# Retention and two feed-forward layers: units of the retention taken in pairs, kind by kind

## The chip, the core and the metric

One core of a Trainium2 chip runs the whole program. Five engines work side by side, each through its own list of instructions in order: TensorE (PE, matmuls into PSUM banks), VectorE (DVE), ScalarE (ACT), GpSimd (POOL) and SyncE (SP, which here only starts DMA transfers). Engines wait for one another on semaphores. The metric is the time of one execution on the device in microseconds; three runs of the kernel before gave 588.07, 588.76 and 588.95 us.

## The reference

```python
def _attn_ref(q, k, v):                   # batch 2, heads 8, seq 768, head_dim 64
    gamma = 1.0 - 2.0 ** (-5.0 - np.arange(H))
    state = np.zeros((B, H, D, D))
    for t in range(S):
        state = gamma * state + outer(k[:, :, t], v[:, :, t])
        y[:, :, t] = D ** -0.5 * q[:, :, t] @ state
...
x = y as (1536 tokens, 512)
x = ((x @ w_a) * (x @ w_b)) @ w_out       # d_ff 1536
h = x @ w_in                              # d_ff 2048
out = np.maximum(0.01 * h, h) @ w_out2
```

The weights are stored in 64-bit floats; x, q, k and v in 32-bit floats.

## The kernel before, in words

The retention is computed in chunks of 128 positions. The 1536 positions (two sequences) are cut into three tiles of 512 positions, four chunks each, and the eight heads into four pairs of heads. One tile of one pair of heads is a **unit**; there are 12, numbered tile by tile, so that units 0 to 3 are the first tile. For a unit four kinds of matmul are run on PE:

- `scores` (L426): k times scaled q inside each chunk, into two PSUM banks (one per head). DVE multiplies each bank with the decay and the causal mask and writes it to SBUF as P (L443, two instructions of 128x512).
- `states` (L454): scaled k (`kd`) times v, into one bank (kv). DVE runs the chain of states through the chunks with three or four small instructions (cr, L476 and L478).
- `within` (L500): P times v, into the bank xp.
- `across` (L514): the spread states times scaled q, added onto xp. Then xp leaves as two tiles, x high (ACT, a rounding copy, L209) and x low (DVE, a subtraction, L210).

Around them stand `prep` (L406): ACT scales n (k in the other layout) to `kd` with two instructions (L415), and GpSimd scales q to `qs` (L419; DVE does it for units 0 and 1); and `spreads` (L483): ACT copies the unit's states into one of two buffers `wk`, whose other halves are zero (L495), so that two heads share one matmul.

Where a matmul has 32-bit operands the trace holds two records for it: 16 for the scores of a unit, 12 or 16 for its states, 16 within, 6 or 8 across.

The loop over u (L626) writes the order by hand, one unit at a time: scores and states of unit u+1, one step of the first weight block, within and across of unit u, spreads of u+1, prep of u+3, loads of u+8. In the last turn but one the spreads of unit 11 stand ahead of within and across of unit 10. Every engine keeps the program's order, so what one function issues on ACT or DVE stands behind all that was issued there before.

`loads` (L390) starts the four transfers q, k, n and v of a unit, 256 KB each, on SP's queue (the first k on ACT's). Each transfer waits on SP until the one eight before it has landed. The loads of units 0 to 6 are issued ahead of the loop. The tiles take slots of one pool of 81 slots of 2 KB per partition, as do kd, qs, P and x.

The weights come in raw blocks of 512 KB of 64-bit floats (`load_weights`, L236, four buffers) and are rounded to 32 bits: ACT makes two parts (`begin_weights`, L255 and L256), DVE joins them in four steps (`round_steps`: sign L270, min L272, shift L274, add L278). `want` then splits the rounded block into a high part (ACT, L209) and a low part (DVE, L210). Only block a0 is rounded inside the loop, in six calls of `micro`: begin; sign; min; shift; add; split. They come one a turn from u = 3 (`EARLY`) on. Its raw transfer is issued between the loads of units 4 and 5 (L614); the next ones are issued at the end of the turns from u = 3 on.

Behind the loop the first layer starts with `pa`: 36 matmuls that read x high, x low, a0 high and a0 low; the third one is the first that reads a0 low. While they run, block b0 is rounded and split, which the next 36 matmuls (pb) read.

Of the kernel before, what the change touches and what calls it, by code (L numbers as in the profile page):

```python
# [19 lines left out]
B, H, S, D = 2, 8, 768, 64  # L20
# [10 lines left out]
NSLOT = 81  # L31
NRAW = 4
NEXTRA = 10
EARLY = 3
NWARM = 7
COUNT = {"a": FF1, "b": FF1, "wo": FF1, "wi": FF2, "wq": FF2}
HALF = FF2 // 2
# [150 lines left out]
def retention_moe_kernel(ctx: ExitStack, tc: tile.TileContext, ins, out):  # L188
    nc = tc.nc
# [10 lines left out]
    def bank(name):  # L200
        return psum.tile([P, TT], F32, tag="ps", name=name)
# [4 lines left out]
    def split(src, name, new=slots.new):  # L206

        hi, lo = new(F32R, name + "h"), new(F32R, name + "l")
        nc.scalar.copy(hi, src)  # L209
        nc.vector.tensor_sub(lo, src, as32(hi))  # L210
        return hi, lo
# [24 lines left out]
    def load_weights():  # L236
        if at["load"] < len(order) and at["load"] < at["round"] + NRAW:
            kind, f = order[at["load"]]
            src, i = source[kind]
            t = rawp.tile([P, TT], I64, tag="raw", name=f"raw_{kind}{f}")  # L240
            nc.sync.dma_start(t, src[f, i])
            raws[kind, f] = t
            at["load"] += 1
# [128 lines left out]
    consts, chain, spread = [], [], []  # L372

    def attention_constants():
        for p in range(NPAIR):
            consts.append(ap.tile([P, P], F32, tag=f"cst{p}", name=f"cst{p}"))

        for p in range(NPAIR):
            chain.append([ap.tile([P, CPT, D], F32, tag=f"cr{p}{j}", name=f"cr{p}{j}") for j in range(2)])

        for i in range(2):
            spread.append(ap.tile([P, CPT, P], F32, tag=f"wk{i}", name=f"wk{i}"))
            nc.gpsimd.memset(spread[i][0:D, :, D:P], 0.0)
            nc.gpsimd.memset(spread[i][D:P, :, 0:D], 0.0)

    units = [(t, p) for t in range(NTILE) for p in range(NPAIR)]
    un = {}
    x = {}

    def loads(u):  # L390
        if u >= len(units):
            return
        t, p = units[u]
        d = un[u] = {}
        if u < NPAIR:
            nc.sync.dma_start(consts[p], grow[p])
        for name, src in (("q", qT), ("k", kT), ("n", kn), ("v", vn)):
            d[name] = slots.new(F32, f"{name}{u}")
            queue = nc.scalar if u == 0 and name == "k" else nc.sync
            queue.dma_start(d[name], src[t, p])  # L400
            if u == 0 and name == "q":
                nc.scalar.dma_start(small, dec)
            if u == 0 and name == "v":
                nc.sync.dma_start(causal, tri)

    def prep(u):  # L406
        if u >= len(units):
            return
        t, p = units[u]
        d = un[u]  # L410
        d["kd"] = slots.new(F32, f"kd{u}")
        for h in range(2):
            o = d["kd"].rearrange("p (j h d) -> p j h d", j=CPT, h=2)[:, :, h, :]
            i = d["n"].rearrange("p (j h d) -> p j h d", j=CPT, h=2)[:, :, h, :]
            nc.scalar.activation(o, i, AF.Copy, scale=small[:, 2 * p + h:2 * p + h + 1])  # L415
        d["qs"] = slots.new(F32, f"qs{u}")
        g = consts[p].rearrange("p (o t) -> p o t", o=1)

        (nc.vector if u < 2 else nc.gpsimd).tensor_mul(  # L419
            d["qs"].rearrange("p (j t) -> p j t", j=CPT),  # L420
            d["q"].rearrange("p (j t) -> p j t", j=CPT),
            g.to_broadcast([P, CPT, P]),
        )
        slots.done(2)

    def scores(u):  # L426

        if u >= len(units):
            return
        t, p = units[u]  # L430
        d = un[u]
        sc = [bank(f"sc{u}{h}") for h in range(2)]
        for j in range(CPT):
            c = slice(j * P, (j + 1) * P)
            for h in range(2):
                r = slice(h * D, (h + 1) * D)
                nc.tensor.matmul(sc[h][:, c], d["k"][r, c], d["qs"][r, c], start=True, stop=True)  # L437
        d["P"] = []
        m = causal.rearrange("p (o t) -> p o t", o=1)
        for h in range(2):  # L440
            pt = slots.new(F32, f"P{u}{h}")
            n = H + NPAIR + 2 * p + h
            nc.vector.scalar_tensor_tensor(  # L443
                pt.rearrange("p (j t) -> p j t", j=CPT),
                sc[h].rearrange("p (j t) -> p j t", j=CPT),
                small[:, n:n + 1],
                m.to_broadcast([P, CPT, P]),
                op0=ALU.mult,
                op1=ALU.mult,
            )  # L450
            d["P"].append(pt)
        slots.done(1)

    def states(u):  # L454
        if u >= len(units):
            return
        t, p = units[u]
        d = un[u]
        kv = bank(f"kv{u}")
        chunks = [t * CPT + j for j in range(CPT)]  # L460
        for j, c in enumerate(chunks):
            if c % CPB != CPB - 1:
                for h in range(2):
                    r = slice(h * D, (h + 1) * D)
                    s = slice(j * P + h * D, j * P + (h + 1) * D)
                    nc.tensor.matmul(
                        kv[r, j * D:(j + 1) * D], d["kd"][:, s], d["v"][:, s], start=True, stop=True
                    )
        own = chain[p][t % 2]
        for j, c in enumerate(chunks):  # L470
            if c % CPB == CPB - 1:
                continue
            o = own[:, j + 1] if j < CPT - 1 else chain[p][(t + 1) % 2][:, 0]
            n = kv[:, j * D:(j + 1) * D]
            if c % CPB == 0:
                nc.vector.tensor_copy(o, n)  # L476
            else:
                nc.vector.scalar_tensor_tensor(  # L478
                    o, own[:, j], small[:, H + p:H + p + 1], n, op0=ALU.mult, op1=ALU.add
                )  # L480
        slots.done(1)

    def spreads(u):  # L483

        if u >= len(units):
            return
        t, p = units[u]
        chunks = [t * CPT + j for j in range(CPT)]
        own = chain[p][t % 2]
        used = [c % CPB != 0 for c in chunks] + [False]  # L490
        runs = [(a, used.index(False, a)) for a in range(CPT) if used[a] and not (a and used[a - 1])]
        for a, b in runs:
            for h in range(2):
                r = slice(h * D, (h + 1) * D)
                nc.scalar.copy(spread[u % 2][r, a:b, h * D:(h + 1) * D], own[r, a:b])  # L495
        un[u]["S"] = spread[u % 2]

    cols = [slice(j * P, (j + 1) * P) for j in range(CPT)]

    def within(u):  # L500
        d = un[u]
        xp = d["x"] = bank(f"xp{u}")
        for j, c in enumerate(cols):
            for h in range(2):
                r = slice(h * D, (h + 1) * D)
                nc.tensor.matmul(
                    xp[r, c],
                    d["v"][:, j * P + h * D:j * P + (h + 1) * D],
                    d["P"][h][:, c],
                    start=j == 0,  # L510
                    stop=False,
                )

    def across(u):  # L514
        t, p = units[u]
        d = un.pop(u)
        xp = d["x"]
        later = [(t * CPT + j) % CPB != 0 for j in range(CPT)]
        for j, c in enumerate(cols):
            if later[j]:  # L520
                nc.tensor.matmul(xp[:, c], d["S"][:, j], d["qs"][:, c], start=False, stop=j == CPT - 1)  # L521
        x[t, p] = split(xp, f"x{u}")
        slots.done(4)


    h = {}
# [83 lines left out]
    for _ in range(NWARM):  # L610
        nc.tensor.matmul(wps, warm[:, 0:P], warm, start=True, stop=True)
    for u in range(1, 7):
        if u == 5:
            load_weights()  # L614
        loads(u)
    prep(0)
    def first_weights():
        begin_weights()
        yield
        yield from round_steps()  # L620
        yield
        want("a", 0)

    micro = first_weights()
    prep(1)
    for u in range(-1, len(units)):  # L626
        scores(u + 1)
        slots.tick()
        if u == 0:
            within(u)  # L630
        states(u + 1)
        slots.tick()
        if u >= EARLY:
            next(micro, None)
        if u + 1 == len(units) - 1:
            spreads(u + 1)
        if u > 0:
            within(u)
        if u >= 0:
            across(u)  # L640
        if u + 1 < len(units) - 1:
            spreads(u + 1)
        if u < 0:
            prep(2)
        else:
            prep(u + 3)
        loads(u + 8)
        if u + 8 >= len(units) - 1:
            load_weights()
        slots.tick()  # L650
    att.close()
# [276 lines left out]
```

## Time and profile before

| | us |
|---|---|
| median of 3 runs | 588.76 (588.07 to 588.95) |
| span of the profiled execution, first to last instruction | 587.1 |
| PE busy | 578.6 (99%) |
| DVE busy | 452.5 (77%) |
| ACT busy | 308.5 (53%) |
| POOL busy | 22.0 (4%) |

The page gives the span of the profiled execution; what lies around the span is in the median and not in the profile. Busy time counts an engine's instructions, not its waits. Matmuls overlap, so the start of one kind to the start of the next says more than a duration. The retention takes the first 50.27 us of the span; the two layers take the rest. In rows of a timeline the columns are the start and the length in us, the engine, the line, the operation, what it writes and reads, the shape and the count; the brackets hold how long the engine was idle before and what released it.

### The profile page before, as it was taken

How to read it: one execution, taken by the hardware profiler on the slowest of the kernel's cores; microseconds unless marked ns; L12 is line 12 of the kernel's file. 1: busy time of each engine (PE TensorE's matmuls, PEld its weight loads, DVE VectorE, ACT ScalarE, POOL GpSimd, SP SyncE). 2: the span in 40 equal slices, each digit the busy share in tenths (PEclk: the TensorE clock that was granted, in tenths of full speed). 3: DMA queues.
4: the chain of work that ended last, by engine and by line, in shares of the span. 5: the costliest groups of instructions: out<-in, count | busy, mean ns of one | idle time of the engine just before them, and what ended most of it. 6: DMA issues, size and time to landing. Idle time of an engine off the chain costs nothing.

```text
span 587.1 us, 8742 instructions
## 1 busy us (share of the span) xinstructions
PE 578.6 (99%) x3247; PEld 488.8 (83%) x3247; DVE 452.5 (77%) x937; ACT 308.5 (53%) x656; POOL 22.0 (4%) x32
## 2 busy tenths in 40 slices
PE   7999999999999999999999999999999999999997
PEld 5788788888888888888888888888888888888886
DVE  4795688889877788889999938657775766879992
ACT  4674446455354344547657356554633356788710
POOL 2430000000000000000000000000000000000000
PEclk9999999999999999999999999999999999999999
DMA  8991244555433343340014102213220000010111
GB/s 306 361 387 47 88 139 151 178 180 179 162 106 124 98 156 116 118 158 22 1 54 143 56 3 105 97 48 107 73 71 2 2 0 1 0 56 1 54 55 54
DMA packets 23050, 59.62 MB, mean 102 GB/s; under 512 B 2784, under 2 KB 4448, under 8 KB 23008
## 3 DMA queue, kind: packets, MB, share of 16 engines
q1 hardware_dynamic: 21600, 55.13, 28.0%
q0 software_dynamic: 1120, 3.67, 1.6%
q8 instruction: 25, 0.41, 0.3%
q10 hardware_dynamic: 288, 0.27, 0.1%
q14 instruction: 17, 0.14, 0.1%
HBM read 52.24 MB, written 6.82 MB: 101 GB/s over the span
## 4 chain that ended last, share of the span: by engine, by line
PE 91%; DMA 4%; DVE 3%; ACT 1%; issue 0%; SPq 0%; DVEq 0%
PE blk L216 11%; PE blk L215 11%; PE blk L217 11%; PE h L215 7%; PE h L216 7%; PE h L217 7%; PE pa L215 5%; PE pa L216 5%; PE pa L217 5%; PE pb L217 5%; PE pb L216 5%; PE pb L215 5%; DMA v<-in_vn 2%; PE xp L521 1%; DMA n<-in_kn 1%; PE sc L437 1%
## 5 line engine op out<-in xcount | busy, mean ns | idle before, releaser
L216 PE MATMUL blk<-form,form 128*128 128x512 f32 (+1 forms) x224 | 75.7, 338 | 0.0
L215 PE MATMUL blk<-form,form 128*128 128x512 f32 (+1 forms) x224 | 75.5, 337 | 0.0
L217 PE MATMUL blk<-form,form 128*128 128x512 f32 (+1 forms) x224 | 75.3, 336 | 0.0
L543 ACT COPY h<-pa 128x512 f32<-128x512 f32 x33 | 19.5, 590 | 84.6 <-PE pa L217 84.6
L779 ACT ACTIVATE g<-h 128x512 f32<-128x512 f32 x48 | 28.6, 597 | 62.2 <-PE h L217 62.2
L138 DVE TENSOR_TENSOR form<-g,form 128x512 fp32r<-128x512 f32 x112 | 57.3, 553 | 2.4 <-ACT form L132 0.7
L216 PE MATMUL blk<-forma,forma 128*128 128x512 f32 (+1 forms) x168 | 57.0, 339 | 0.4 <-DVE forma L138 0.4
L132 ACT CAST form<-g 128x512 fp32r<-128x512 f32 x112 | 52.6, 514 | 8.4 <-DVE g L113 6.4
L215 PE MATMUL blk<-forma,forma 128*128 128x512 f32 (+1 forms) x168 | 56.6, 337 | 0.0
L217 PE MATMUL blk<-forma,forma 128*128 128x512 f32 (+1 forms) x168 | 56.5, 336 | 0.0
L138 DVE TENSOR_TENSOR form<-wq,form 128x256 fp32r<-128x256 f32 x56 | 23.6, 421 | 35.5 <-ACT form L132 35.4
L215 PEld LDWEIGHTS blk<-form,form 128*128 128x128 f32 x224 | 42.5, 190 | 5.5
L216 PEld LDWEIGHTS blk<-form,form 128*128 128x128 f32 x224 | 42.5, 190 | 5.0
L217 PEld LDWEIGHTS blk<-form,form 128*128 128x128 f32 x224 | 42.3, 189 | 4.7
L138 DVE TENSOR_TENSOR forma<-h,forma 128x512 fp32r<-128x512 f32 x84 | 43.1, 553 | 0.8
L132 ACT CAST forma<-h 128x512 fp32r<-128x512 f32 x84 | 38.8, 511 | 0.0
L216 PEld LDWEIGHTS blk<-forma,forma 128*128 128x128 f32 x168 | 31.8, 189 | 4.6 <-DVE forma L138 0.9
L215 PEld LDWEIGHTS blk<-forma,forma 128*128 128x128 f32 x168 | 31.8, 190 | 4.1
L217 PEld LDWEIGHTS blk<-forma,forma 128*128 128x128 f32 x168 | 31.7, 189 | 3.5
L113 DVE TENSOR_TENSOR g<-g,g 128x512 f32<-128x512 f32 (+1 forms) x56 | 30.7, 571 | 3.6 <-ACT g L779 3.6
L546 DVE TENSOR_TENSOR h<-h,pb 128x512 f32<-128x512 f32 x33 | 22.5, 683 | 8.4 <-PE pb L217 5.4
L132 ACT CAST forma<-wo 128x256 fp32r<-128x256 f32 x42 | 17.1, 407 | 17.4 <-PE blk L217 13.2
(3091 smaller groups left out, 1447.3 us busy)
## 6 DMA issues: line engine op xcount, KB each, us to landing
raw_wi<-in_w SPq DMA_DIRECT2D x16, 512.0 KB, 3.2
raw_wq<-in_w SPq DMA_DIRECT2D x16, 512.0 KB, 3.4
raw_a<-in_wab SPq DMA_DIRECT2D x12, 512.0 KB, 3.2
raw_b<-in_wab SPq DMA_DIRECT2D x12, 512.0 KB, 3.4
raw_wo<-in_wo SPq DMA_DIRECT2D x12, 512.0 KB, 3.3
q<-in_qT SPq DMA_DIRECT2D x12, 256.0 KB, 5.2
n<-in_kn SPq DMA_DIRECT2D x12, 256.0 KB, 5.2
v<-in_vn SPq DMA_DIRECT2D x12, 256.0 KB, 5.3
```

The costliest lines, as they stand in the source:

```text
L113: queue.append((cost, lambda piece=piece: run(*(self.A(*x[1:], j)[piece] for x in (d, x0, x1)))))
L132: nc.scalar.copy(h, src)
L138: nc.vector.tensor_sub(*todo.pop(0))
L215: nc.tensor.matmul(ps, w[0], x[0], start=first, stop=False, skip_group_check=more)
L216: nc.tensor.matmul(ps, w[0], x[1], start=False, stop=False, skip_group_check=more)
L217: nc.tensor.matmul(ps, w[1], x[0], start=False, stop=last, skip_group_check=more)
L437: nc.tensor.matmul(sc[h][:, c], d["k"][r, c], d["qs"][r, c], start=True, stop=True)
L521: nc.tensor.matmul(xp[:, c], d["S"][:, j], d["qs"][:, c], start=False, stop=j == CPT - 1)
L543: nc.scalar.copy(h[t, f], pa)
L546: nc.vector.tensor_mul(h[t, f], h[t, f], pb)
L779: nc.scalar.activation(g[t, f], ps, AF.Lrelu, alpha=0.01)
```

## The change

From unit 4 (`SINGLE`) on, units are taken in pairs. A turn n of the loop has a group `now` and the following group `then`, of one unit up to unit 3 and of two units behind it. Scores of both units of `then` come first, then the states of both, then within for both units of `now`, then across for both. In a turn whose `then` is a pair, the preparation (`prep`) up to two units beyond `then` is issued between within and across; otherwise it stays at the end of the turn. The spreads of `then` follow across, but in the last turn that has a `then` they stand ahead of that preparation and of across. There are four spread buffers instead of two. The six steps of block a0 come two a turn, behind across and the spreads, from the turn of units 4 and 5 on. The raw transfer of a0 is issued behind the loads of unit 9; loads run seven units ahead of `now` instead of eight.

```diff
-        for i in range(2):
+        for i in range(4):
             spread.append(ap.tile([P, CPT, P], F32, tag=f"wk{i}", name=f"wk{i}"))
...
     for u in range(1, 7):
-        if u == 5:
-            load_weights()
         loads(u)
...
-    for u in range(-1, len(units)):
-        scores(u + 1)
+    groups = [[u] for u in range(SINGLE)] + [[u, u + 1] for u in range(SINGLE, len(units), 2)]
+    prepared = 2
+    for n in range(-1, len(groups)):
+        now = groups[n] if n >= 0 else []
+        then = groups[n + 1] if n + 1 < len(groups) else []
+        for u in then:
+            scores(u)
         slots.tick()
-        if u == 0:
-            within(u)
-        states(u + 1)
+        if n == 0:
+            within(0)
+        for u in then:
+            states(u)
         slots.tick()
-        if u >= EARLY:
-            next(micro, None)
-        if u + 1 == len(units) - 1:
-            spreads(u + 1)
-        if u > 0:
-            within(u)
-        if u >= 0:
-            across(u)
-        if u + 1 < len(units) - 1:
-            spreads(u + 1)
-        if u < 0:
-            prep(2)
-        else:
-            prep(u + 3)
-        loads(u + 8)
-        if u + 8 >= len(units) - 1:
-            load_weights()
+        if n > 0:
+            for u in now:
+                within(u)
+        last = n + 2 == len(groups)
+        if last:
+            for u in then:
+                spreads(u)
+        if len(then) == 2:
+            while prepared <= then[-1] + 2:
+                prep(prepared)
+                prepared += 1
+        for u in now:
+            across(u)
+        if not last:
+            for u in then:
+                spreads(u)
+        while prepared <= (then or now)[-1] + 2:
+            prep(prepared)
+            prepared += 1
+        if now and now[0] >= SINGLE:
+            next(micro, None)
+            next(micro, None)
+        for u in now:
+            loads(u + 7)
+            if u == 2:
+                load_weights()
+        if now and now[-1] + 7 >= len(units):
+            load_weights()
         slots.tick()
```

`spreads` takes buffer `u % 4` where it took `u % 2`.

## Rows read from the trace of the kernel before

**Rows 1.** The page, busy time of each engine: us, share, instructions.

```profile
PE 578.6 (99%) x3247; PEld 488.8 (83%) x3247; DVE 452.5 (77%) x937; ACT 308.5 (53%) x656; POOL 22.0 (4%) x32
```

**Rows 2.** The chain of waits, 10 to 30 us: start, length, what.

```profile
16.13 7.49 DMA n<-in_kn
...
26.72 1.02 PE xp L521 x6
```

**Rows 3.** Timeline of PE, 33 to 51 us.

```profile
33.47 0.94 PE L521 MATMUL xp<-qs,wk 128*128 128x128 f32 x6
34.34 1.16 PE L437 MATMUL sc<-qs,k 64*128 64x128 f32 x16
...
37.67 1.16 PE L437 MATMUL sc<-qs,k 64*128 64x128 f32 x16
...
43.69 1.16 PE L521 MATMUL xp<-qs,wk 128*128 128x128 f32 x8
...
50.27 0.47 PE L215 MATMUL pa<-x0h,a0h 128*128 128x512 f32 x1
...
50.81 0.40 PE L217 MATMUL pa<-x0h,a0l 128*128 128x512 f32 x1
```

**Rows 4.** Stretches: length, busy (PE, PEld, DVE, ACT, POOL; second PE alone), clock, DMA, GB/s.

```profile
30.00:45.00 15.00, 15.00 (x218) 13.09 (x216) 14.55 (x33) 10.54 (x28) 5.12 (x4) 1.00 0.97 370
...
584.20:587.10 2.90, 0.00 (x0) 1.00 0.50 176
```

**Rows 5.** Timeline of DVE, 31 to 50 us.

```profile
31.76 0.42 DVE L272 TENSOR_SCALAR a<-a 128x512 f32<-128x512 f32 x1
32.10 0.68 DVE L210 TENSOR_TENSOR x5l<-xp,x5h 128x512 fp32r<-128x512 f32 x1
...
37.99 0.68 DVE L278 CUSTOM_DVE_ANT_0 a<-a,low 128x1024 uint16<-128x1024 uint16 x1
38.59 0.69 DVE L210 TENSOR_TENSOR x7l<-xp,x7h 128x512 fp32r<-128x512 f32 x1
...
40.51 0.90 DVE L478 SCALAR_TENSOR_TENSOR cr<-cr,small,kv 128x64 f32<-128x64 f32 x3
41.33 0.69 DVE L210 TENSOR_TENSOR a0l<-a,a0h 128x512 fp32r<-128x512 f32 x1
42.00 0.69 DVE L210 TENSOR_TENSOR x8l<-xp,x8h 128x512 fp32r<-128x512 f32 x1
42.61 1.40 DVE L443 SCALAR_TENSOR_TENSOR P<-sc,small,causal 128x512 f32<-128x512 f32 x2
43.92 0.90 DVE L478 SCALAR_TENSOR_TENSOR cr<-cr,small,kv 128x64 f32<-128x64 f32 x3
...
49.95 0.69 DVE L210 TENSOR_TENSOR x10l<-xp,x10h 128x512 fp32r<-128x512 f32 x1 [1.56 <-ACT x10h L209]
```

**Rows 6.** Timeline of ACT, 23 to 50 us.

```profile
23.64 0.91 ACT L415 ACTIVATE kd<-n,small 128x256 f32<-128x256 f32 x2 [1.99 <-DMA n<-in_kn]
...
39.11 0.91 ACT L415 ACTIVATE kd<-n,small 128x256 f32<-128x256 f32 x2
39.92 0.60 ACT L209 CAST a0h<-a 128x512 fp32r<-128x512 f32 x1
...
41.86 0.83 ACT L495 COPY wk<-cr 64x256 f32<-64x256 f32 x2
42.72 0.91 ACT L415 ACTIVATE kd<-n,small 128x256 f32<-128x256 f32 x2
...
49.33 0.59 ACT L209 CAST x10h<-xp 128x512 fp32r<-128x512 f32 x1
```

**Rows 7.** Timeline of SP, loads of unit 11.

```profile
32.81 1.04 SPq L400 DMA_DIRECT2D q<-in_qT  x1
34.66 0.33 SPq L400 DMA_DIRECT2D k<-in_kT  x1
35.34 0.33 SPq L400 DMA_DIRECT2D n<-in_kn  x1
```

**Rows 8.** DMA issues, 35.2 to 35.6 us: count, KB each, us to landing.

```profile
n<-in_kn SPq DMA_DIRECT2D x1, 256.0 KB, 5.3
```

More of the change, by code (lines that the diff above doesn't have):

```diff
@@ L33 @@
 NEXTRA = 10
-EARLY = 3
+SINGLE = 4
 NWARM = 7
@@ L494, in spreads @@
                 r = slice(h * D, (h + 1) * D)
-                nc.scalar.copy(spread[u % 2][r, a:b, h * D:(h + 1) * D], own[r, a:b])
-        un[u]["S"] = spread[u % 2]
+                nc.scalar.copy(spread[u % 4][r, a:b, h * D:(h + 1) * D], own[r, a:b])
+        un[u]["S"] = spread[u % 4]
     cols = [slice(j * P, (j + 1) * P) for j in range(CPT)]
```

## Prediction

> **What bounds the kernel now.** The page comes first: TensorE (PE) is busy for 578.6 of 587.1 us [rows 1], so a change can win or lose only where PE waits or works inefficiently. The chain of waits shows where PE is not the chain: a DMA up to 23.6 us, ScalarE (ACT) up to 26.7, and from there PE [rows 2] until the retention ends at 50.27, where the first matmul of the first layer (pa) starts [rows 3]. Everything behind 50.27 is the same program in both kernels. So the sum is made at that point: what pa's matmuls lose or gain there is the result, if nothing behind gives it back.
>
> The table of engine times by stretch comes next: from 30 to 45 us PE is busy 15.00 of 15 us, VectorE (DVE) 14.55, and the DMA engines 0.97 of the time at 370 GB/s [rows 4]. Three resources run at their limit side by side. A unit takes PE 3.33 us (scores at 34.34 to scores at 37.67 [rows 3]); it takes DMA 1.05 MB / 370 GB/s = 2.8 us; it takes DVE 1.31 for P, 0.82 for the chain and 0.61 for x low, 2.74 us [rows 5], and in this stretch the steps of the first weight block besides. So little can be bought on PE alone.
>
> The timelines of single engines come last. ACT works in order, and one row shows what hurts there: the scaled keys kd of unit 5 stood 1.99 us waiting for the DMA of n [rows 6], and all that is queued behind on ACT (x high, the spreads) stood with them.
>
> **The change part by part.** *Raw block a0 later.* It is 0.52 MB, 1.4 us at 370 GB/s. It stands ahead of unit 5 now and will stand ahead of unit 10. So the inputs of units 5 to 9 land some 1.3 us earlier. For unit 11 nothing changes: the same bytes are ahead of it in the one queue, and that queue is never short of work there [rows 4]. I therefore keep the landing of n of unit 11: issued at 35.34, landed 5.3 later, at 40.6 us [rows 7, 8]. The raw block lands ahead of that by all of unit 10 and q, k and n of unit 11, 1.8 MB or 4.9 us: near 36.
>
> *Units in pairs.* A change of kind on PE costs something fixed. The products with the states (across) have 6 records in 0.94 us and 8 in 1.16, 0.11 a record; 6 of them take 0.87 from start to the next kind's start (33.47 to 34.34), so about 0.21 is fixed. Scores, 1.16 as well, are like the 8 [rows 3], and get the same. For state updates and products within a chunk I can separate nothing: between 0 and 0.21 each, and I take 0, as these two follow each other with the same array form. Four pairs save one change of each kind: 4 x 0.42 = 1.7 us (up to 3.4). This counts only if PE is what ends last.
>
> *Two units prepared ahead of the x casts of a turn.* In a pair's turn ACT gets kd of two further units before x high and the spreads. Those casts then wait for DMA, where now they wait for PE. The turn of unit 3 runs kd6 and kd7 first, that of 4 and 5 kd8 and kd9, that of 6 and 7 kd10 and kd11. DVE is in order too: x low stands behind x high and ahead of the next P. So each late landing stops ACT, then DVE. kd5 started at 23.64 on its landing [rows 6]; less 1.3, and two units of 2.7 to 2.8 on, kd7 starts near 27.7 and x3 high 0.81 behind it, so that DVE, which by its own work is through with the chain of unit 5 near 26, idles some 3 us. The same comes before x4 low (under 1 us) and x6 low (over 1). DVE has 2.74 of every 3.33 us to do and can't make these up.
>
> *The last turns, step by step,* from one start to the next in the rows [rows 5, 6]:
> - kd11 starts when n of unit 11 has landed, 40.7; x6 high 0.81 behind it (as 39.11 to 39.92), 41.5. Its product on PE was ready long before.
> - x6 low 0.62 behind that (as 49.33 to 49.95), 42.1; x7 low 0.6 on, 42.7; then two steps of the weight block: min at 43.3, 0.34 long (as 31.76 to 32.10), and the shift, which I price like the add at 0.60. P10 starts at 44.25.
> - P10 1.31, P11 1.31, the chain of unit 10 0.82 and that of unit 11 0.9 to its end: 48.6.
> - The code puts the spreads of 10 and 11 ahead of x8 high here, and the spread of 11 needs that chain: 48.7, 0.86 long (as 41.86 to 42.72). x8 high at 49.5.
> - x8 low 50.15, x9 low 50.75, and only now the last rounding step of the block, the add: 51.35, ready 0.68 later, at 52.05.
> - a0 high on ACT 52.1, 0.60 long; a0 low on DVE 52.7, 0.69 long: ready at 53.4.
>
> PE ends the retention at about 50.4 in the same walk. The saved changes of kind go into a wait: the scores of 11 need the scaled q, whose tile lands two transfers ahead of n, near 39.2, and takes GpSimd 1.28 (5.12 for 4 [rows 4]), so they start at 40.6; then come 1.16 of scores, two state updates of 0.4, and within and across of four units, 4 x (0.95 + 1.08). Then pa needs a0: its third matmul, which reads a0 low, starts at 53.45 in place of 50.81 [rows 3]. That is +2.65 us. Now a0 low is ready at 42.0 (41.33 and 0.69 [rows 5]), eight microseconds before its use; this cover is gone, and it is what is late next.
>
> *Four spread buffers.* GpSimd clears four more halves at the start, while the first inputs are still on their way, and its first product is that of unit 2. Nothing; a bound is 0.3 us, one clear. They also take away a wait of the spreads for the unit two before, which no row shows as a stall.
>
> *Loads a turn later.* SP isn't in step with PE here: it issues when an earlier transfer lands (0.68 from k to n of unit 11, as long as a transfer takes [rows 7]). Unit 11's tiles now take slots used before, of units long done. Nothing; a bound is 0.7 us, one transfer, if a slot comes free late.
>
> *Behind the retention.* b0's rounding follows x11 low on DVE in both. Its five steps there are of 0.34 to 0.7 us [rows 5], under 4 us with their casts on ACT, and 36 matmuls of pa at over 0.2 us, more than 7 us, are ahead of its use. So the shift passes on whole. The sum is +2.65 us: the profiled span of 587.1 becomes 589.75. The median of the runs, 588.76, lies 1.7 above that span, for what lies around it; with the same 1.7 comes 591.4.
>
> **The rivals.** *Faster: PE is what counts.* If DVE and ACT kept step with PE, the pairs would bring their 1.7 us. The point from which this decides is a0 low ready by 49 us, over 4 us ahead of my walk. For it: PE had no break from 26.7 on. Against: n of unit 11 lands at 40.6, and the order of the code puts 12.8 us of ACT and DVE steps one behind the other from there to a0 low. Time: 587.1.
>
> *No change: DMA runs earlier.* From q to k of unit 11 SP stood 1.85 us, 1.2 more than from k to n [rows 7]: the transfers paused there once. If that pause falls behind unit 11 in the new order, the whole chain starts 1.2 us sooner; a transfer rate 4% higher over the 40 us would give up to 1.6. Then +1.05 to +1.45, 589.8 to 590.2, on the edge of no change.
>
> *Slower still: the clock falls.* PE idles some 2.3 us ahead of a0. In the kernel's last 2.9 us no matmul ran and the granted clock stayed at 1.00, its 2.4 GHz level [rows 4], so I expect none of it. If it fell to 1.2 GHz for half of pa's opening 8 us, that would be 2 us more: 593.4. The Trainium skill, page TensorE: Matmul & The Clock Gate, Part 1 (the HAM clock gate), has an idle array fall back to the lower level; by that rule alone this would be the forecast, but the row of the kernel's end doesn't bear it out for a gap of this size.
>
> *The change doesn't do what it says:* kinds stand in pairs in the program, yet the second scores may wait for their q, and PE is no faster. That is in the forecast, at 50.4.
>
> **How the numbers follow.** The forecast has 0.68, the faster rival 0.06, no change 0.16, the clock 0.10. About 0.2%, 1.2 us, is what a measurement of this kernel can tell from no change, so slower begins at 589.95. Half of the no-change rival lies below that edge, and the forecast's lower tail (n landing over 1.4 earlier) adds 0.06: faster 0.06, same 0.14, slower 0.80. The range runs from an early DMA to a fallen clock, 589.4 to 593.4.
>
> **What would show it.** Right: pa's first matmuls wait for a0 high and low at 52 to 53.5, PE idle for about 2 us ahead of them; DVE idle near 26 to 29 for x3 low; kd7, kd9 and kd11 waiting for the DMA of n; the add of a0 behind x9 low; the scores of a pair back to back. Wrong: a0 low ready before 50 us, n of unit 11 landed before 39, or DVE busy throughout from 26 to 45.

## The result and the profile after

The changed kernel takes 591.64 us (median; 590.28 to 592.57) against 588.66 for the kernel before in the same comparison: ratio 1.0051, interval 1.0036 to 1.0066. It is slower by 3.0 us (2.1 to 3.9). The profiled execution took 591.91 us with a span of 590.0, 2.9 us over the span of before. One execution of a later experiment, at 639.77 us and a granted clock of 0.852 over its whole span, is left out of its median.

Where the 2.9 us come in is seen on PE. This is the timeline of PE in the changed kernel, from the first pair on to the first layer; it answers to [rows 3].

```profile
19.44 1.16 PE L437 MATMUL sc<-qs,k 64*128 64x128 f32 x16
21.64 1.16 PE L437 MATMUL sc<-qs,k 64*128 64x128 f32 x16 [1.04 <-POOL qs L419]
...
27.03 1.16 PE L437 MATMUL sc<-qs,k 64*128 64x128 f32 x16 [0.55 <-POOL qs L419]
...
30.72 1.60 PE L521 MATMUL xp<-qs,wk 128*128 128x128 f32 x12
32.25 2.06 PE L437 MATMUL sc<-qs,k 64*128 64x128 f32 x32
34.24 0.92 PE L466 MATMUL kv<-v,kd 128*64 128x64 f32 x24
34.99 1.92 PE L506 MATMUL xp<-P,v 128*64 128x128 f32 x32
36.84 1.60 PE L521 MATMUL xp<-qs,wk 128*128 128x128 f32 x12
38.37 2.29 PE L437 MATMUL sc<-qs,k 64*128 64x128 f32 x32
...
47.57 2.05 PE L521 MATMUL xp<-qs,wk 128*128 128x128 f32 x16 [0.18 <-ACT wk L495]
51.60 0.75 PE L215 MATMUL pa<-x0h,a0h 128*128 128x512 f32 x1 [1.98 <-ACT a0h L209]
52.15 0.63 PE L216 MATMUL pa<-x0l,a0h 128*128 128x512 f32 x1
52.58 0.63 PE L217 MATMUL pa<-x0h,a0l 128*128 128x512 f32 x1
```

From the third pair on the pairs do what they say: scores of two units are one block of 32 records, and a whole round of two units takes 6.12 us (32.25 to 38.37) where two single ones took 6.66. PE is through with the retention at 49.62 (47.57 + 2.05), 0.65 ahead of the time at which pa started before. Then it stands still for 1.98 us, released by a0 high. The third matmul of pa starts at 52.58 instead of 50.81.

DVE shows the chain that leads there. The timeline of DVE in the changed kernel answers to [rows 5]; note the brackets (idle time before, and the releaser) and the place of the add (L278).

```profile
28.87 0.69 DVE L210 TENSOR_TENSOR x3l<-xp,x3h 128x512 fp32r<-128x512 f32 x1 [3.35 <-ACT x3h L209]
...
34.15 0.69 DVE L210 TENSOR_TENSOR x4l<-xp,x4h 128x512 fp32r<-128x512 f32 x1 [0.67 <-ACT x4h L209]
...
40.79 0.69 DVE L210 TENSOR_TENSOR x6l<-xp,x6h 128x512 fp32r<-128x512 f32 x1 [0.74 <-DMA raw_a<-in_wab]
...
43.06 2.72 DVE L443 SCALAR_TENSOR_TENSOR P<-sc,small,causal 128x512 f32<-128x512 f32 x4
45.69 1.73 DVE L478 SCALAR_TENSOR_TENSOR cr<-cr,small,kv 128x64 f32<-128x64 f32 x6
49.01 0.69 DVE L210 TENSOR_TENSOR x8l<-xp,x8h 128x512 fp32r<-128x512 f32 x1 [1.59 <-ACT x8h L209]
49.62 0.68 DVE L210 TENSOR_TENSOR x9l<-xp,x9h 128x512 fp32r<-128x512 f32 x1
50.22 0.68 DVE L278 CUSTOM_DVE_ANT_0 a<-a,low 128x1024 uint16<-128x1024 uint16 x1
51.58 0.69 DVE L210 TENSOR_TENSOR a0l<-a,a0h 128x512 fp32r<-128x512 f32 x1 [0.68 <-ACT a0h L209]
```

The bracket of x6 low names a DMA, but that block was issued at 28.80 and landed 5.9 us later; x6 high ends at 40.76, and x6 low starts at 40.79.

ACT, which answers to [rows 6], waits for n ahead of the x casts, three times in three turns (kd7, kd9 and kd11):

```profile
27.46 0.91 ACT L415 ACTIVATE kd<-n,small 128x256 f32<-128x256 f32 x2 [2.23 <-DMA n<-in_kn]
28.27 0.56 ACT L209 CAST x3h<-xp 128x512 fp32r<-128x512 f32 x1
...
32.74 0.91 ACT L415 ACTIVATE kd<-n,small 128x256 f32<-128x256 f32 x2 [0.73 <-DMA n<-in_kn]
33.55 0.56 ACT L209 CAST x4h<-xp 128x512 fp32r<-128x512 f32 x1
...
39.38 0.91 ACT L415 ACTIVATE kd<-n,small 128x256 f32<-128x256 f32 x2 [0.47 <-DMA n<-in_kn]
40.20 0.56 ACT L209 CAST x6h<-xp 128x512 fp32r<-128x512 f32 x1
...
46.68 1.68 ACT L495 COPY wk<-cr 64x256 f32<-64x256 f32 x4 [3.86 <-DVE cr L478]
48.39 0.58 ACT L209 CAST x8h<-xp 128x512 fp32r<-128x512 f32 x1
```

The n that the last of these kd waits for is that of unit 11. SP issued it at 33.61, and the list of DMA issues has it land 5.7 later, at 39.3; before it was 40.6 [rows 7, 8].

```profile
32.70 0.35 SPq L400 DMA_DIRECT2D q<-in_qT  x1
33.15 0.36 SPq L400 DMA_DIRECT2D k<-in_kT  x1
33.61 0.39 SPq L400 DMA_DIRECT2D n<-in_kn  x1
```

```profile
n<-in_kn SPq DMA_DIRECT2D x1, 256.0 KB, 5.7
```

The 1.98 us are not the whole loss in this execution. Pa's matmuls come 0.43 us apart at first, not 0.23. The table of PE by stretch (length, busy time and count, granted clock, DMA share, GB/s) has two stretches of one length:

```profile
51.70:55.00 3.30, 3.30 (x8) 0.50 0.03 11
55.20:58.50 3.30, 3.30 (x16) 1.00 0.33 129
```

Right behind the idle time the granted clock is 0.50, the 1.2 GHz level, and half as many matmuls run. a0 low is ready at 52.27 (51.58 + 0.69), which alone would put the third matmul at 52.3, 1.5 us late. The last of pa's 36 starts 2.96 us late, so about 1.45 us are the clock's in this execution. From there on nothing is given back: the last matmul of the kernel ends 2.88 us later than before.

### The profile page after: what moved, and what is told of

Its sections match the earlier page's. It is cut to its first block, busy times and chain, and to the rows that moved or that the text cites. A ratio compares the mean times of both kernels' runs of the same rounds, so it can differ in the third digit from the quotient of the medians.

```text
span 590.0 us, 8741 instructions
## 1 busy us (share of the span) xinstructions
PE 579.0 (98%) x3247; PEld 489.7 (83%) x3247; DVE 452.4 (77%) x937; ACT 308.1 (52%) x656; POOL 23.2 (4%) x36
## 4 chain that ended last, share of the span: by engine, by line
PE 89%; DMA 6%; DVE 3%; ACT 1%; SPq 0%; issue 0%; DVEq 0%; ACTq 0%
PE blk L216 11%; PE blk L215 11%; PE blk L217 11%; PE h L215 7%; PE h L216 7%; PE h L217 7%; PE pa L215 6%; PE pa L216 6%; PE pa L217 6%; PE pb L217 5%; PE pb L216 5%; PE pb L215 5%; DMA n<-in_kn 3%; DMA v<-in_vn 2%; DMA k<-in_kT 1%; DMA raw_a<-in_wab 1%
```

## Experiments

Times are medians in us against the kernel before in the same comparison, with the ratio's 95% interval.

**The split ahead of the x casts.** The changed kernel; add and split of a0 are issued ahead of across in the last turn with a follower.

```diff
+        if last:
+            next(micro, None)
+            next(micro, None)
         for u in now:
             across(u)
...
-        if now and now[0] >= SINGLE:
+        if now and now[0] >= SINGLE and not last:
             next(micro, None)
             next(micro, None)
```

> The changed kernel with one edit: in the last turn that has a following pair, the last two steps of block a0 (add and split) are issued ahead of across and the x casts of units 8 and 9 instead of behind them. Theory A (a0's split stands behind x8 and x9 low in the last turn, and that alone makes the first layer wait): a0 low is ready near 49.8 us instead of 52.3, about when PE ends the retention (49.6 before, x8 and x9 low now 1.3 us later, which nothing waits for at once); PE's 2.0 us gap ahead of pa is under 0.5 us, the granted clock stays at 1.00 through pa; pa's third matmul at 50.0 to 50.4; 0.4 to 0.8 us less than the kernel before, some 588.1, and 3 to 3.5 us less than the changed kernel. Rival B (the pairs themselves are slower, because ACT and DVE wait for DMA): still 1 us or more above the kernel before. Rival C (the late raw block a0 is what is late): no gain against the changed kernel.

588.41 against 588.70, ratio 0.9992 (0.9983 to 1.0001): no slower than before, and 3.2 us under the changed kernel's median, though short of the gain of 0.4 to 0.8 us that I expected. In its profiled execution, which at 587.77 us is faster than its median, the timeline of DVE has the add ahead of x8 low, and pa starts without an idle time of note:

```profile
47.01 0.69 DVE L278 CUSTOM_DVE_ANT_0 a<-a,low 128x1024 uint16<-128x1024 uint16 x1
48.71 0.69 DVE L210 TENSOR_TENSOR a0l<-a,a0h 128x512 fp32r<-128x512 f32 x1 [1.02 <-ACT a0h L209]
49.32 0.68 DVE L210 TENSOR_TENSOR x8l<-xp,x8h 128x512 fp32r<-128x512 f32 x1
```

```profile
49.05 0.47 PE L215 MATMUL pa<-x0h,a0h 128*128 128x512 f32 x1
49.36 0.39 PE L216 MATMUL pa<-x0l,a0h 128*128 128x512 f32 x1
49.59 0.39 PE L217 MATMUL pa<-x0h,a0l 128*128 128x512 f32 x1
```

So the place of two steps in the program carries the whole loss; the pairs and the late raw block stayed, and rivals B and C fall.

**Idle time filled.** The changed kernel with eight matmuls that nothing reads between the retention and pa.

```diff
         slots.tick()
+    fill = bank("fill")
+    for _ in range(8):
+        nc.tensor.matmul(fill, warm[:, 0:P], warm, start=True, stop=True)
     att.close()
```

> The changed kernel with eight matmuls of the warm-up kind (128x512 bf16, into a bank that nothing reads) between the retention and pa. Theory A with the clock as a second term: the wait for a0 stays (a0 high ready at about 51.5, pa's first matmul there), but the granted clock stays at 1.00 through pa in every execution, which takes away the 1.6 us that pa lost between 51.7 and 55.1 in the profiled execution; executions between +1.2 and +2.4 us against the kernel before, median some 590.3. If the fall of the clock has nothing to do with the idle array, the clock falls here too in about half of the executions and the median stays at 591.6.

590.87 against 588.70, 1.0039 (1.0027 to 1.0051). Four of the five executions show a mean granted clock of 1.000 (590.31 to 591.24 us); the fifth, the profiled one, shows 0.95 over its whole span and no fall behind the retention. In the changed kernel two of four executions show 0.997, which is what 3.4 us at half clock make of 590; these two took 591.91 and 592.57, the two at 1.000 took 590.28 and 591.38. The matmuls of the execution at 0.95 come 0.23 us apart as in the others, so what that figure records is open. With the array filled no execution shows the fall; these are few executions, and the two intervals overlap, so the time that it saves, about 0.7 us in the median, is not shown by the timing alone.

The profile also shows the wait by itself. Here kd11 waited for its n until 40.54, and the third matmul of pa starts 2.68 us later than before with no fall:

```profile
40.54 0.91 ACT L415 ACTIVATE kd<-n,small 128x256 f32<-128x256 f32 x2 [0.95 <-DMA n<-in_kn]
```

```profile
53.49 0.50 PE L217 MATMUL pa<-x0h,a0l 128*128 128x512 f32 x1
```

**The raw block back.** The changed kernel with a0's transfer ahead of unit 5 again.

```diff
     for u in range(1, 7):
+        if u == 5:
+            load_weights()
         loads(u)
...
-            if u == 2:
-                load_weights()
```

> The changed kernel with the raw transfer of a0 where it was, between the loads of units 4 and 5; all else as changed. Theory A: n of unit 11 lands at the same time, so the chain from there is the same; a0 low ready within 0.8 us of the changed kernel, and the time within 1 us of it: 591 to 592.5. Rival C (the late raw block is the cause): 2 us or more faster than the changed kernel, back at 588.7.

591.96 against 588.70, 1.0057 (1.0044 to 1.0071). The late block is not the cause. But a0 low was ready at 54.1, 1.85 us later than in the changed kernel, where I had put it within 0.8. The trace shows where the time went: the scores of 5 wait 2.82 us for their q, the array idles, and the clock falls right there:

```profile
19.60 1.16 PE L437 MATMUL sc<-qs,k 64*128 64x128 f32 x16
23.58 2.08 PE L437 MATMUL sc<-qs,k 64*128 64x128 f32 x16 [2.82 <-POOL qs L419]
```

```profile
23.00:30.00 7.00, 6.42 (x62) 0.51 1.02 355
```

That is what the raw move is for in a program of pairs: two scores in a row ask for unit 5's q a unit's time earlier. Here kd10 and kd11 run from 40.42 on without a wait for n, so in this run the last turns hang on what ACT had to do before, and not on the landing. The gap ahead of pa is 0.52 us, with the clock at 1.00 behind it.

**The raw move alone.** The kernel before, units singly, a0's transfer behind the loads of unit 9, its steps in the turns of 7, 8, 9 (two) and 10 (two).

```diff
-EARLY = 3
+STEPS = {7: 1, 8: 1, 9: 2, 10: 2}
...
     for u in range(1, 7):
-        if u == 5:
-            load_weights()
         loads(u)
...
-        if u >= EARLY:
+        for _ in range(STEPS.get(u, 0)):
             next(micro, None)
...
-        if u + 8 >= len(units) - 1:
+        if u == 1 or u + 8 >= len(units) - 1:
             load_weights()
```

> The kernel before with the raw move alone: units singly, a0's transfer behind the loads of unit 9, and its six steps later to suit (one in the turn of unit 7, one in 8, two in 9, two in 10). Theory A: the inputs of units 5 to 9 come 1.3 us earlier, PE reaches the scores of 5 at 22.4 instead of 23.7, and the end of the retention comes earlier by up to that, less what the later steps cost DVE: pa's third matmul 0.5 to 1.2 us earlier than before, 587.6 to 588.2. If the early data is worth nothing (PE bound by DVE), no change within 0.3 us; if the later steps of a0 hurt as they do in the changed kernel, 1 us slower.

589.01 against 588.70, 1.0007 (0.9998 to 1.0017): a miss, no gain. The scores of 11 start 1.40 us earlier than before (43.37, where it was 44.77). But ACT has the split's cast ahead of unit 11's spreads, and across of unit 11 waits for these:

```profile
47.88 0.62 ACT L209 CAST a0h<-a 128x512 fp32r<-128x512 f32 x1 [3.08 <-DVE a L278]
48.40 0.83 ACT L495 COPY wk<-cr 64x256 f32<-64x256 f32 x2
```

```profile
49.28 1.16 PE L521 MATMUL xp<-qs,wk 128*128 128x128 f32 x8 [1.26 <-ACT wk L495]
```

What the early data earned was paid back through the last two of the six steps, this time by way of the spreads.

**n of unit 11 later.** The changed kernel with raw block b0 also ahead of unit 10.

```diff
             if u == 2:
                 load_weights()
+                load_weights()
```

> The changed kernel with raw block b0 also moved ahead of the loads of unit 10, so that units 10 and 11 land 1.3 us later; nothing else. Theory A (the last turns are one chain of ACT and DVE steps that starts at the landing of n of unit 11): a0 low ready 1.3 us later than in the changed kernel at the same DMA pauses, 12.8 to 13.0 us behind that landing as there (52.27 - 39.30), and the time up by about 1.3, near 592.9. Rival (the sum of DVE's work from unit 4 on sets the end, not the landing): a0 low and the time as in the changed kernel, 591.6.

593.45 against 588.47, 1.0087 (1.0073 to 1.0100): 1.8 us more than the changed kernel's median in its own comparison. n of unit 11 landed at 40.6 (issued at 34.69, 5.9 to landing), kd11 started on it, and a0 low was ready at 53.55:

```profile
40.66 0.91 ACT L415 ACTIVATE kd<-n,small 128x256 f32<-128x256 f32 x2 [1.77 <-DMA n<-in_kn]
```

```profile
42.07 0.69 DVE L210 TENSOR_TENSOR x6l<-xp,x6h 128x512 fp32r<-128x512 f32 x1 [2.13 <-ACT x6h L209]
...
52.86 0.69 DVE L210 TENSOR_TENSOR a0l<-a,a0h 128x512 fp32r<-128x512 f32 x1 [0.68 <-ACT a0h L209]
```

From the start of kd11 to a0 low it is 12.89 us here (40.66 to 53.55) and 12.89 in the changed kernel (39.38 to 52.27); in the filled version, with the same transfers as the changed kernel, it is 12.90 (40.54 to 53.44). The landing moved by 1.3 us and a0 low with it; a sum of DVE's work would not have moved. Four of five executions show the clock's 0.997, more than in the changed kernel, which is where the rest of the 1.8 can come from; that was not tried.

**Behind unit 7, singly.** The kernel before with a0's transfer behind the loads of unit 7 and `EARLY` 5.

```diff
-EARLY = 3
+EARLY = 5
...
-        if u == 5:
-            load_weights()
         loads(u)
...
-        if u + 8 >= len(units) - 1:
+        if u == -1 or u + 8 >= len(units) - 1:
             load_weights()
```

> The kernel before with the raw transfer of a0 behind the loads of unit 7 and its six steps two turns later (from u = 5, one a turn); units singly. Theory A: units 5 to 7 land 1.3 us earlier, scores of 5 start at 22.4, ACT is not held by the block's first step ahead of x3 high, PE runs at 3.33 us a unit from there; a0 low is ready at 47.4, ahead of its use; pa's third matmul 1.2 to 1.6 us earlier: 587.1 to 587.5. If DVE, which is within 0.1 us a unit of PE, eats it: 588.4 to 588.7.

587.77 against 588.47, 0.9987 (0.9979 to 0.9996). Faster, by half of what I expected. In its profile, whose 587.20 us are faster than the median, PE has no idle time over 0.1 us from 8.2 us to the first layer, so nothing but PE's own work is left there.

**The last pair alone.** The changed kernel with `SINGLE` 10, a0's transfer behind the loads of unit 6, and its steps in the turns of 5 (two), 7, 8 and, ahead of across, 9 (two). It has two runs; the profile is that of the second.

```diff
-SINGLE = 4
+SINGLE = 10
+STEPS = {5: 2, 7: 1, 8: 1}
...
     for u in range(1, 7):
         loads(u)
+    load_weights()
...
+        if last:
+            next(micro, None)
+            next(micro, None)
         for u in now:
             across(u)
...
-        if now and now[0] >= SINGLE:
-            next(micro, None)
+        for _ in range(STEPS.get(n, 0)):
             next(micro, None)
...
-            if u == 2:
-                load_weights()
```

> The changed kernel with the last two units alone as a pair (SINGLE 10), the raw transfer of a0 behind the loads of unit 6, its steps begin and sign in the turn of unit 5, min in 7, shift in 8, add and split in 9 ahead of across. Theory A: the data comes early as in the run above, no kd of a pair stands ahead of x casts while its DMA is on the way, and the one pair saves one change of each kind (0.4 to 0.5 us): pa's third matmul 1.6 to 2.1 us earlier than before, 586.6 to 587.1, under both kernels. If a pair brings nothing of itself: as the run above, 587.1 to 587.5.

> The version with the last two units alone as a pair once more, for a profile in the undisturbed state: pa's third matmul near 48.8 us, no gap of PE over 0.3 us between 24 us and pa, a0 low ready near 48.3; 586.6 to 587.1.

586.88 against 588.47, 0.9972 (0.9961 to 0.9982), and 586.97 against 588.72, 0.9970 (0.9958 to 0.9982). It beats both kernels, the one before by 1.6 and by 1.75 us. From 8.0 us on PE is busy for 39.54 of 39.60 us up to pa (kernel before: 40.61 of 42.27 up to 50.27):

```profile
8.00:47.60 39.60, 39.54 (x606) 1.00 0.93 344
```

**No pair.** The same with `SINGLE` 12, and add and split ahead of across of unit 10 (`n == 10` for `last`).

> The same version without any pair (SINGLE 12): units 10 and 11 singly, add and split of a0 ahead of across of unit 10; raw transfer, preparation and all else the same. If the pair of the last two units brings something of itself (one change of each kind saved, 0.5 us): 0.4 to 0.6 us slower than with it, 587.2 to 587.6. If the whole gain is in the raw block's place: the same as with it.

587.67 against 588.72, 0.9982 (0.9973 to 0.9991), 0.7 us behind the version with one pair in the same comparison; the intervals overlap a little. The profiles settle how much of it is the pair. From the scores of 9 to pa it takes 12.12 us with the pair (first fence) and 12.60 without (second):

```profile
35.49 1.16 PE L438 MATMUL sc<-qs,k 64*128 64x128 f32 x16
...
47.61 0.48 PE L216 MATMUL pa<-x0h,a0h 128*128 128x512 f32 x1
```

```profile
36.26 1.16 PE L438 MATMUL sc<-qs,k 64*128 64x128 f32 x16
...
48.86 0.47 PE L216 MATMUL pa<-x0h,a0h 128*128 128x512 f32 x1
```

These 0.48 us are about the one change of each kind that a pair saves (6.66 - 6.12 = 0.54 us), where no data is late. The 0.77 us by which the second profile is already late at the scores of 9 stand ahead of the pair, where the two programs have the same order.

## Why the prediction was right, and where it was lucky

The mechanism held at every step: kd6 and kd7, kd8 and kd9, kd10 and kd11 stood ahead of the x casts, and kd7, kd9 and kd11 waited there for n; DVE idled 3.35 us ahead of x3 low (some 3 predicted), 0.67 ahead of x4 low (under 1) and 0.74 ahead of x6 low (over 1 predicted); the spreads stood ahead of x8 high, the add behind x9 low, and pa waited for a0. Moving only the two last steps gave the loss back, and moving only the landing moved a0 low by as much. That the place of the preparation ties a0 to that landing is read from the order of the rows; no run puts only the preparation back behind across.

The size, 591.4 for a measured 591.64, is in part luck: in the profiled execution two misses cancel. The chain from the landing of n of unit 11 to a0 low was put at 12.8 us and took 13.0. But its start was put at 40.6, as before, and was 39.3: between q and k of unit 11, where [rows 7] have 1.85 us, SP took 0.45. That is the condition of the rival "no change", which had 0.16. So the wait itself cost 1.5 us, not 2.65. The other part, about 1.45 us, is the rival to which I gave 0.10: the clock fell behind the idle time. It fell in two of four executions, and its price was put at 2 us.

Other executions divide it otherwise. The profile of the filled version has the sum as I made it: kd11 on its landing at 40.54, pa's third matmul 2.68 us late where 2.65 were forecast, and no fall. The two executions of the changed kernel without a fall were 1.6 and 2.7 us over the median before. The two profiles show that the landing differs with the same transfers, and the times without a fall spread as widely; the median near the forecast holds executions of both kinds.

The argument against a fall of the clock failed. It rested on the kernel's end, where 2.9 us without a matmul kept the clock at 1.00 [rows 4]; a gap of 1.98 us in the middle was followed by 0.50. No run shows what sets the two gaps apart. The rule of the Trainium skill, page TensorE: Matmul & The Clock Gate, Part 1, that the array falls to the lower level after idling, was the better guide to the direction: the trace agrees, with 0.50 from 51.7 to 55.0, though the fall came in two executions of four only. The page does not settle a gap of this size, so "by that rule alone this would be the forecast" went further than it does.

The walk had PE through at 50.4, where its own terms add to 50.7 (40.6 + 1.16 + 0.8 + 8.12); it was 49.6, for the same early landing: GpSimd was through with the q of unit 11 at 39.45, which the walk had near 40.5. The sum of 2.65 us does not rest on that time; the idle time of PE does, put at 2.3 us and measured at 1.98. Of the saving of a pair I had 0.42 us, from two changes of kind of 0.21; measured are 0.54, of which scores give 0.19 (1.99 against 2 x 1.09), across 0.21 (1.53 against 2 x 0.87), and within and states the rest, where I had put nothing. Four pairs at 0.54 would be 2.2 us. PE waited for q instead (1.04 and 0.55 us), so that the scores of 4 and 5 and of 6 and 7 did not stand back to back, and what was left by 49.6 went into the wait for a0. No row shows a cost of the loads, the spread buffers or the stretch behind pa, as forecast; none of them was tried alone.

## What to carry to other kernels

When work is grouped to make one engine's order better, look at what the grouping puts ahead of what on the other in-order engines: an instruction that waits for a DMA holds back everything behind it, and a step that had eight microseconds of cover can end up last in line. Count from the last landing along the program's order, engine by engine, to the first instruction of the next stage. And place small side work by what it stands in front of: the same two steps cost 3 us in one place, made PE wait for 1.26 us in a second, and cost nothing in a third.

## What the runs showed of the hardware

- In the changed kernel's profile a gap of PE of 1.98 us behind the retention was followed by the 1.2 GHz level. Mean clocks of 0.997 say the same of two of four executions here and of four of five with the later landing; gaps of 0.6 us in the kernel before were not followed by it. It cost 1.45 us, where the wait itself cost 1.5. One execution of the split ahead of the x casts shows 0.996; it is not the profiled one, so where the clock fell in it is open.
- The pauses of DMA come and go: n of unit 11 landed at 40.6 before and at 39.3 in the changed kernel with the same bytes ahead of it, and with the same transfers kd11 had to wait until 40.54 in the filled version. That is 0.2% of the kernel, as much as is to be decided here. What makes the pauses was not tried.
